# A linear-attention and mixture kernel: the state update's products spread over all four quarters of TensorE's array

## The chip, the cores and the metric

The kernel runs on one core of a Trainium2 chip. The metric is the device time of one launch in microseconds (us), as the median of several runs. The engines are TensorE (PE in the rows, with PEld for its weight loads), VectorE (DVE), ScalarE (ACT), GpSimd (POOL) and SyncE (SP), which here only issues transfers. Each engine works through a stream of its own in a fixed order and waits on semaphores for the others.

## The reference, cut to what matters

Three parts follow each other. The first is a recurrence over 768 tokens for 4 batches (b) and 8 heads (h), with a 48x48 state for each of the 32 pairs:

```python
for t in range(S):                       # S = 768, D = 48
    kt, vt, bt = (k_n[:, :, t], v[:, :, t], beta[:, :, t, None])
    y[:, :, t] = np.einsum('bhd,bhde->bhe', q[:, :, t], state)
    v_old = np.einsum('bhde,bhd->bhe', state, kt)
    state = state + bt[:, :, :, None] * np.einsum('bhd,bhe->bhde', kt, vt - v_old)
```

Its output, 3072 rows of 384, goes through `h = (x @ w1) * (x @ w2) @ w3` and `h @ w_out` (width 1024), and then through a soft mixture of 8 experts with 4 slots each: softmax over the tokens, two expert matrices, softmax over the slots. Everything is float32 in the reference.

## The kernel before

**Tiling of the recurrence.** The 768 tokens are 24 chunks n of 32 tokens; two neighbours form a pair c (12 pairs). Within a chunk the recurrence is solved as a triangular system (`solve_steps`, mostly VectorE); from chunk to chunk the state is carried. `chain_steps(n)` (lines 579 to 648) holds the steps of one chunk, in this order: `pre` (GpSimd scales v), `ks` (L599, keys times state, then a subtraction on VectorE, L601), `vv` (L610, the solved system times v, then four ScalarE copies, L575, into the tile `sv`), `yy` (L620, queries times state, output `yp`, copied by ScalarE, L623), `ss` (L630, only in the second chunk of a pair, and not in the last pair: 11 times in all) and `xt` (L642, transposes for the next part).

**The state.** `sv` has 128 rows and a block of 384 columns (8 heads of 48) for each batch. Batches 0 and 1 keep their state in rows 64 to 111, batches 2 and 3 in rows 0 to 47 (`srow`); the other rows hold the chunk's solved v, of batches 0 and 1 in rows 0 to 63 and of batches 2 and 3 in rows 64 to 127. The sum of the state itself stays in two accumulators of PSUM, `sacc[0]` for batches 0 and 2 and `sacc[1]` for batches 1 and 3. `ss` adds 32 products to them (4 batches, 8 heads, each 64 rows deep with 48 columns in and out), and then ScalarE copies each batch's part of the accumulator into its rows of `sv` (four copies of 48x384, L575). One product in the program is two weight loads and two matmuls in the trace, so `ss` is 64 records of each.

**A product's place in the array.** A product that reads rows 0 to 63 uses the upper half of the array's rows, one that reads 64 to 127 the lower half; its output rows in PSUM, 0 to 47 or 64 to 111, set which half of the columns it uses. So a quarter of the array is a pair of such halves. `yy` and `vv`, by contrast, write 32 output rows for each batch, so that the four batches take four strips of 32 columns.

**The work around it.** `main_steps(c)` runs the two big matrices on the 64 tokens of a pair: `prod` (L695, output `ab`, 18 matmuls of 128x256 for each of 8 blocks), ScalarE and VectorE (L699, L704) for the product of both, `gtr` (L712) transposes, then logits, softmax and sums (L719 to L798). In the first 205 us VectorE, ScalarE and GpSimd also convert the weights w1, w2, w3 and w_out from 64-bit to 32-bit pieces (L290 to L307), and TensorE multiplies w3 and w_out with phi (L322 to L356). After about 580 us comes a tail with the experts.

**What sets the order.** The steps are entered with due times (`when`, `spread`, a table `SHIFT`), and a scheduler that simulates the engines then decides each engine's order from the dependencies. A step that takes another time in its simulation, or waits for something else, can move its neighbours.

Of the kernel before, what the change touches and what calls it, by code (L numbers as in the profile page):

```python
# [19 lines left out]
B, H, S, D = 4, 8, 768, 48  # L20
# [3 lines left out]
NCH = NST // 2  # L24
# [96 lines left out]
def kern(ctx, tc, kq, vt, kt, bl, w12, w3, wo, phi, w1e, w2e, consts, out):  # L121
    nc = tc.nc
    V, A, G, T = nc.vector, nc.scalar, nc.gpsimd, nc.tensor
# [25 lines left out]
    def at(name):  # L149
        return bank("at", 2, name)  # L150
# [23 lines left out]
    sv = px.tile([128, 4, H * D], F32, name="sv")  # L174
    sacc = [ps.tile([128, 512], F32, name=f"sacc{i}") for i in range(2)]
# [19 lines left out]
    def kl_of(p):  # L195

        i = p if p < 3 else (0, 1, 3, 2)[(p - 3) % 4]
        return held4 if i == 3 else kls[i]
# [27 lines left out]
    def srow(b):  # L226

        return slice(64, 112) if b < 2 else slice(0, 48)

    def qrow(b):  # L230
        return slice(32 * b, 32 * b + 32)

    def trow(n, b):

        return qrow(b if n % 2 else b ^ 1)

    def kcol(h, b):
        return slice(64 * h + 32 * (b % 2), 64 * h + 32 * (b % 2) + 32)
# [171 lines left out]
    def g_step(n, hs, which="gp"):  # L410

        s, n4 = divmod(n, 4)
        if n4 == 0 and "g" in which and hs[0] == 0:
            Dg[s] = pk.tile([128, 32, 32], F32, tag="L", name=f"dg{s}", bufs=NL)
        t = kl_of(n // 2)
        k = [(3, 3), (5, 1)][n % 2]

        span = {"gp": [((3, 7), (0, 4)), ((5, 7), (0, 2))], "g": [((3, 4), (3, 4)), ((5, 6), (1, 2))],
                "p": [((4, 7), (0, 3)), ((6, 7), (0, 1))]}[which][n % 2]
        nb = span[0][1] - span[0][0]  # L420
        p = (ab if n // 4 == 1 else at)(f"{which}{n}_{hs[0]}")
        gp = p[:, 0:len(hs) * nb * 32].rearrange("p (h k i) -> p h k i", h=len(hs), k=nb)
        for h in hs:
            for b in range(4):
                r, kc, j = srow(b), kcol(h, b), b // 2
                lo, hi = span[j]
                slots = slice(lo, hi) if j == 0 else slice(hi - 1, lo - 1 if lo else None, -1)
                T.matmul(gp[trow(n, b), h - hs[0]], lhsT=t[r, k[j], kc], rhs=t[r, slots, kc], start=True, stop=True)  # L428
        blocks = {}
        if "g" in which:  # L430
            blocks["g"] = 0
        if "p" in which:
            blocks["p"] = o = len(which) - 1
            blocks["x"] = o + 1
        g_evac(n, hs, gp, blocks, n < PP)
# [134 lines left out]
    def copy(n, b, o, i):  # L570

        if n < NSPLIT and b % 2:
            V.tensor_copy(o, i)
        else:
            A.copy(o, i)  # L575

    def chain_steps(n):
        s, n4 = divmod(n, 4)
        c, t2 = divmod(n, 2)
        st = {}  # L580
        kl = kl_of(n // 2)

        def pre():
            v = KV[n]
            G.tensor_tensor(out=v, in0=v, in1=nnT[s][:, 8 * n4:8 * n4 + 8].unsqueeze(2).to_broadcast([128, H, D]),  # L585
                            op=ALU.mult)

        def rows(b):
            return slice(0, 112) if b < 2 else slice(0, 128)

        def ks():

            v = KV[n]
            p = at(f"ks{n}")
            kp = p[:, 0:384].rearrange("p (h d) -> p h d", h=H)
            for h in range(H):
                for b in range(4):
                    r, o = (rows(b) if t2 else srow(b)), trow(n, b)
                    T.matmul(kp[o, h], lhsT=kl[r, (5, 1)[b // 2] if t2 else 3, kcol(h, b)],  # L599
                             rhs=sv[r, b, h * D:(h + 1) * D], start=True, stop=True, tile_position=(r.start, o.start))  # L600
            V.tensor_tensor(out=v, in0=v, in1=kp, op=ALU.subtract)  # L601

        def vv():
            r, w = KV[n], W[s]
            assert s not in HALVES or n4 in joined[s]
            p = at(f"vp{n}")
            for h in range(H):
                for b in range(4):
                    o = qrow(b)
                    T.matmul(p[o, h * D:(h + 1) * D], lhsT=w[o, 8 * n4 + h, :], rhs=r[o, h, :],  # L610
                             start=True, stop=True, tile_position=(o.start, o.start))
            for b in (0, 2, 1, 3):
                copy(n, b, sv[trow(n, b), b, :], p[trow(n, b), 0:384])

        def yy():
            p = at(f"yp{n}")
            for h in range(H):
                for b in range(4):
                    r = trow(n, b) if n == 0 else rows(b)
                    T.matmul(p[qrow(b), h * D:(h + 1) * D], lhsT=kl[r, (6, 0)[b // 2] if t2 else (4, 2)[b // 2], kcol(h, b)],  # L620
                             rhs=sv[r, b, h * D:(h + 1) * D], start=True, stop=True, tile_position=(r.start, 32 * b))
            ys = px.tile([128, DM], F32, tag="ys", name=f"ys{n}", bufs=2)
            A.copy(ys, p[:, 0:384])  # L623
            st["y"] = ys

        def ss():
            k = KK[c]
            for h, b in [(h, b) for b2 in range(2) for h in range(H) for b in (b2, b2 + 2)]:
                r = slice(64 * (b // 2), 64 * (b // 2) + 64)
                T.matmul(sacc[b % 2][srow(b), h * D:(h + 1) * D], lhsT=k[r, b % 2, h, :],  # L630
                         rhs=sv[r, b, h * D:(h + 1) * D], start=False, stop=(c == NCH - 2),
                         skip_group_check=True, tile_position=(r.start, 64 - 64 * (b // 2)))
            for b in (0, 2, 1, 3):
                copy(n, b, sv[srow(b), b, :], sacc[b % 2][srow(b), 0:384])

        def xt():
            ys = st["y"]
            if t2 == 0:
                xT[c] = [pl["xt"].tile([128, 3, 2, 128], F32R, tag="xT", name=f"xT{c}_{i}", bufs=4) for i in range(2)]
            p = (at if n < NXT else tr)(f"xp{n}")  # L640
            for k in range(3):
                T.transpose(p[:, k * 128:(k + 1) * 128], ys[:, k * 128:(k + 1) * 128], ident)  # L642
            xh, xl = xT[c]
            pv = p[:, 0:384].rearrange("p (k t) -> p k t", k=3)
            A.copy(xh[:, :, t2, :], pv)  # L645
            V.tensor_tensor(out=xl[:, :, t2, :], in0=pv, in1=xh[:, :, t2, :].bitcast(F32), op=ALU.subtract)  # L646

        return [pre] + [ks] * (n > 0) + [vv, yy] + [ss] * (t2 and c < NCH - 1) + [xt]
# [272 lines left out]
    for c in range(NCH):  # L921
        a, b, p = main_steps(c)
# [117 lines left out]
    for hf in range(2):  # L1040
        p = ab(f"h1p{hf}")
        for f in range(8):
            q = 32 * (f % 4)
            T.matmul(p[q:q + 32], lhsT=uT[:, f % 4, f // 4, :], rhs=w3s[hf][f],
                     start=(f < 4), stop=(f >= 4), skip_group_check=True)
# [19 lines left out]
    for f in range(8):  # L1065
        q = 32 * (f % 4)
        m = T.matmul(p[q:q + 32, 0:384], lhsT=h1T[:, f, :], rhs=wos[:, f, :], start=(f < 4), stop=(f >= 4),
                     skip_group_check=True)
    load_w2(nfree + 4, nlate)
    si = u4[:, 0:DM]  # L1070
    for k in range(3):
        c = slice(k * 128, (k + 1) * 128)
# [201 lines left out]
```

## Time and profile before

| | before |
|---|---|
| time, median of 3 runs | 643.93 us (643.07 to 649.51) |
| the profiled execution: its time / its span | 642.53 / 640.7 us |
| TensorE busy: matmuls / weight loads | 548.9 / 458.8 us |
| VectorE, ScalarE, GpSimd busy | 400.3, 278.6, 161.8 us |
| mean granted TensorE clock | 0.946 |

A group of equal instructions has its busy time, the mean duration of one, and the idle time of its engine just ahead of it with what ended that. A matmul's duration in the records is its latency, and several are in flight at once: what a group costs the engine is read from the time between its first start and the next group's start. In the timeline, a row is a run of equal instructions: its start, its length, the engine and line, output and inputs, and the count.

### The profile page before, as it was taken

How to read it: one execution, taken by the hardware profiler on the slowest of the kernel's cores; microseconds unless marked ns; L12 is line 12 of the kernel's file. 1: busy time of each engine (PE TensorE's matmuls, PEld its weight loads, DVE VectorE, ACT ScalarE, POOL GpSimd, SP SyncE). 2: the span in 40 equal slices, each digit the busy share in tenths (PEclk: the TensorE clock that was granted, in tenths of full speed). 3: DMA queues.
4: the chain of work that ended last, by engine and by line, in shares of the span. 5: the costliest groups of instructions: out<-in, count | busy, mean ns of one | idle time of the engine just before them, and what ended most of it. 6: DMA issues, size and time to landing. Idle time of an engine off the chain costs nothing.

```text
span 640.7 us, 25996 instructions
## 1 busy us (share of the span) xinstructions
PE 548.9 (86%) x11417; PEld 458.8 (72%) x11417; DVE 400.3 (62%) x1257; ACT 278.6 (43%) x704; POOL 161.8 (25%) x215
## 2 busy tenths in 40 slices
PE   5324546888899799899999999897999999999996
PEld 4323435887777688679888888786989899886464
DVE  3996899998667115994379826997982313134124
ACT  1515644245574436454444455343444454333023
POOL 0726858334254016232030113004010000000100
PEclk9999666598999989999999999999999999999997
DMA  9904234446843720310404030122344130788848
GB/s 205 332 4 146 81 83 144 130 130 204 254 151 129 164 70 17 87 45 18 105 7 96 9 90 30 38 61 63 106 145 155 63 108 2 268 274 318 344 160 265
DMA packets 36945, 81.72 MB, mean 128 GB/s; under 512 B 4352, under 2 KB 17792, under 8 KB 35584
## 3 DMA queue, kind: packets, MB, share of 16 engines
q1 hardware_dynamic: 36832, 80.07, 40.9%
q8 instruction: 89, 1.46, 1.0%
q14 instruction: 24, 0.20, 0.1%
HBM read 69.57 MB, written 10.49 MB: 125 GB/s over the span
## 4 chain that ended last, share of the span: by engine, by line
PE 55%; DVE 26%; issue 6%; DMA 5%; POOL 4%; ACT 3%; SPq 0%; DVEq 0%; POOLq 0%; ACTq 0%
PE ab L695 24%; DMA kl<-kq 4%; PE gp L712 3%; PE yp L620 3%; DVE xl L512 2%; PE vp L610 2%; DVE tmp L509 2%; PE sacc L630 2%; PE gp L428 2%; PE ks L599 2%; PE sacc L1119 2%; PE hp L1098 2%; DVE gl L454 2%; DVE xl L487 1%; PE lp L719 1%
## 5 line engine op out<-in xcount | busy, mean ns | idle before, releaser
L695 PE MATMUL ab<-xT,wsl 128*128 128x256 f32 x1728 | 247.1, 296 | 3.6 <-DVE gT L704 2.2
L695 PEld LDWEIGHTS ab<-xT,wsl 128*128 128x128 f32 x1728 | 221.8, 196 | 15.6 <-issue 6.3
L704 DVE TENSOR_TENSOR gT<-ab,bs 128x256 f32<-128x256 f32 x84 | 35.2, 422 | 87.3 <-ACT bs L699 79.0
L699 ACT COPY bs<-ab 128x256 f32<-128x256 f32 x96 | 35.7, 371 | 68.0 <-PE ab L695 66.3
L585 POOL TENSOR_TENSOR v<-v,nnT 128x384 f32<-128x384 f32 x24 | 21.4, 894 | 139.2 <-DMA v<-vt 57.0
L575 ACT COPY sv<-vp 32x384 f32<-32x384 f32 x96 | 45.1, 470 | 16.2 <-PE vp L610 14.5
L512 DVE TENSOR_TENSOR xl<-xl,tmp 128x84 f32<-128x84 f32 (+35 forms) x220 | 51.5, 266 | 0.7
L509 DVE TENSOR_TENSOR tmp<-xl 128x84 f32<-128x84 f32 (+35 forms) x220 | 49.6, 259 | 0.4
L428 PE MATMUL gp<-kl 48*32 48x64 f32 (+1 forms) x1024 | 35.7, 275 | 11.7 <-ACT kl L408 8.6
L299 POOL TENSOR_TENSOR hold<-hold 128x384 f32<-128x384 f32 (+1 forms) x32 | 32.7, 1025 | 47.9 <-DVE hold L296 23.0
L428 PEld LDWEIGHTS gp<-kl 48*32 48x32 f32 x1024 | 26.1, 121 | 17.8 <-ACT kl L408 8.9
L713 ACT COPY gtok<-gp 128x512 f32<-128x512 f32 x48 | 28.2, 588 | 17.2 <-PE gp L712 15.0
L393 POOL TENSOR_TENSOR kl<-praw,cs 64x256 f32<-64x256 f32 x28 | 25.3, 903 | 33.5 <-ACT praw L384 32.3
L620 PE MATMUL yp<-sv,kl 112*32 112x48 f32 (+2 forms) x1280 | 26.3, 215 | 7.6 <-ACT sv L575 7.6
L291 ACT ACTIVATE hold<-hold,cs 128x384 int32<-128x384 int32 (+1 forms) x32 | 18.7, 589 | 27.7 <-DVE hold L290 27.3
L408 ACT COPY kl<-gp 32x256 f32<-32x256 f32 x64 | 23.2, 363 | 15.0 <-DVE kl L393 11.8
L620 PEld LDWEIGHTS yp<-sv,kl 112*32 112x32 f32 (+2 forms) x1280 | 20.4, 115 | 12.2 <-issue 8.4
L610 PE MATMUL vp<-v,w 32*32 32x48 f32 x1536 | 25.3, 207 | 3.1 <-DVE mst L738 0.9
L646 DVE TENSOR_TENSOR xT<-xp,xT 128x384 fp32r<-128x384 f32 x24 | 13.3, 553 | 22.8 <-ACT xT L645 22.6
L610 PEld LDWEIGHTS vp<-v,w 32*32 32x32 f32 x1536 | 20.1, 107 | 10.2 <-issue 6.0
L712 PE MATMUL gp<-cs,gT 128*128 128x128 f32 x168 | 26.9, 279 | 0.0
L400 POOL TENSOR_TENSOR kl<-praw,cs 32x256 f32<-32x256 f32 x28 | 23.2, 828 | 7.7 <-ACT praw L384 4.8
(248 smaller groups left out, 980.6 us busy)
## 6 DMA issues: line engine op xcount, KB each, us to landing
hold<-w SPq DMA_DIRECT2D x16, 384.0 KB, 3.3
v<-vt SPq DMA_DIRECT2D x24, 192.0 KB, 2.7
kk<-kt SPq DMA_DIRECT2D x12, 384.0 KB, 6.7
unitg<-w1e SPq DMA_DIRECT2D x6, 768.0 KB, 5.7
kl<-kq SPq DMA_DIRECT2D x8, 512.0 KB, 6.8
kl<-kq SPq DMA_DIRECT2D x8, 384.0 KB, 4.6
gx<-w SPq DMA_DIRECT2D x4, 768.0 KB, 8.2
raw_w<-w SPq DMA_DIRECT2D x4, 768.0 KB, 8.8
```

The costliest lines, as they stand in the source:

```text
L299: G.tensor_tensor(out=w, in0=m, in1=w, op=ALU.mult)
L428: T.matmul(gp[trow(n, b), h - hs[0]], lhsT=t[r, k[j], kc], rhs=t[r, slots, kc], start=True, stop=True)
L509: V.tensor_tensor(out=tmp[:, 0:n, lo:hi], in0=x[:, j + 1:32, j:j + 1].to_broadcast([128, n, hi - lo]), in1=x[:, j:j + 1, lo:hi].to_broadca ...
L512: V.tensor_tensor(out=x[:, j + 1:32, lo:hi], in0=x[:, j + 1:32, lo:hi], in1=tmp[:, 0:n, lo:hi], op=ALU.add)
L575: A.copy(o, i)
L610: T.matmul(p[o, h * D:(h + 1) * D], lhsT=w[o, 8 * n4 + h, :], rhs=r[o, h, :], start=True, stop=True, tile_position=(o.start, o.start))
L620: T.matmul(p[qrow(b), h * D:(h + 1) * D], lhsT=kl[r, (6, 0)[b // 2] if t2 else (4, 2)[b // 2], kcol(h, b)], rhs=sv[r, b, h * D:(h + 1) * D ...
L695: T.matmul(o, lhsT=w[:, m, k], rhs=x[:, k], start=(n == 0), stop=(n == 8))
L699: A.copy(bs, p[:, 256:512])
L704: V.tensor_tensor(out=gt, in0=p[:, 0:256], in1=bs, op=ALU.mult)
L712: T.transpose(p[:, t * 256 + i * 128:t * 256 + (i + 1) * 128], gt[:, t * 128:(t + 1) * 128], ident)
L713: A.copy(gk, p)
```

## The change

```diff
+    def arow(b):
+
+        return srow(b if b % 2 == 0 else 3 - b)
...
         def ss():
             k = KK[c]
-            for h, b in [(h, b) for b2 in range(2) for h in range(H) for b in (b2, b2 + 2)]:
-                r = slice(64 * (b // 2), 64 * (b // 2) + 64)
-                T.matmul(sacc[b % 2][srow(b), h * D:(h + 1) * D], lhsT=k[r, b % 2, h, :],
-                         rhs=sv[r, b, h * D:(h + 1) * D], start=False, stop=(c == NCH - 2),
-                         skip_group_check=True, tile_position=(r.start, 64 - 64 * (b // 2)))
+            for h in range(H):
+                for b in (0, 2, 1, 3):
+
+                    r, o = slice(64 * (b // 2), 64 * (b // 2) + 64), arow(b)
+                    T.matmul(sacc[b % 2][o, h * D:(h + 1) * D], lhsT=k[r, b % 2, h, :],
+                             rhs=sv[r, b, h * D:(h + 1) * D], start=False, stop=(c == NCH - 2),
+                             skip_group_check=True, tile_position=(r.start, o.start))
             for b in (0, 2, 1, 3):
-                copy(n, b, sv[srow(b), b, :], sacc[b % 2][srow(b), 0:384])
+                copy(n, b, sv[srow(b), b, :], sacc[b % 2][arow(b), 0:384])
```

Before, batches 0 and 1 used the quarter (upper rows, right columns) and batches 2 and 3 the quarter (lower rows, left columns), and all products of `sacc[0]` stood ahead of those of `sacc[1]`. Now batch 1 is summed in rows 0 to 47 of `sacc[1]` and batch 3 in rows 64 to 111, so they use the two quarters that stood idle, and the four batches of a head are entered one after the other. The ScalarE copies of batches 1 and 3 read one half of the partitions and write the other. Number and size of products and copies stay as they were. Lines behind the insertion move down by four, behind the loop by six (L630 is L636, L620 is L624, L695 is L701).

The scheduler makes the following of it. The first place is `ss` of pair 8 on TensorE (the names end in numbers: `kk_6997` are the keys of that pair, `sacc_109` is `sacc[0]`, `sacc_110` is `sacc[1]`; x16 is 16 products). Before:

```order
L620 MATMUL yp_7482<-sv,kl_112 32x48
L630 MATMUL sacc_109<-sv,kk_6997 48x48 x3
L620 MATMUL yp_7482<-sv,kl_112 32x48 x2
L630 MATMUL sacc_109<-sv,kk_6997 48x48
L620 MATMUL yp_7482<-sv,kl_112 32x48 x29
L630 MATMUL sacc_109<-sv,kk_6997 48x48 x12
L630 MATMUL sacc_110<-sv,kk_6997 48x48 x16
L642 MATMUL xp_7583<-cs,ys_7515 128x128 x3
```

The same place now:

```order
L624 MATMUL yp_7482<-sv,kl_112 32x48
L636 MATMUL sacc_109<-sv,kk_6997 48x48 x4
L624 MATMUL yp_7482<-sv,kl_112 32x48 x31
L636 MATMUL sacc_110<-sv,kk_6997 48x48 x4
L636 MATMUL sacc_109<-sv,kk_6997 48x48 x2
L636 MATMUL sacc_110<-sv,kk_6997 48x48 x2
L636 MATMUL sacc_109<-sv,kk_6997 48x48 x2
L636 MATMUL sacc_110<-sv,kk_6997 48x48 x2
L636 MATMUL sacc_109<-sv,kk_6997 48x48 x2
```

The pattern of two and two goes on to the end of `ss`, 24 products in all: pairs on one diagonal of quarters alternate with pairs on the other. Pairs 9 and 10 read the same.

The second place is `ss` of pair 1 on TensorE, while w3 is still being multiplied with phi (`w3tw`). Before:

```order
L630 MATMUL sacc_109<-sv,kk_1288 48x48 x5
L343 MATMUL w3tw_1725<-cs,hold 128x128 x3
L630 MATMUL sacc_109<-sv,kk_1288 48x48 x9
L356 MATMUL w3tw_1685<-cs,part_1657 128x32
L630 MATMUL sacc_109<-sv,kk_1288 48x48
```

Now:

```order
L636 MATMUL sacc_109<-sv,kk_1288 48x48 x5
L347 MATMUL w3tw_1725<-cs,hold 128x128 x3
L636 MATMUL sacc_109<-sv,kk_1288 48x48 x9
L360 MATMUL w3tw_1685<-cs,part_1657 128x32
L636 MATMUL sacc_109<-sv,kk_1288 48x48
```

Nothing moved here: one accumulator is still filled almost whole ahead of the other, because the products of batches 0 and 2 are ready earlier. Pair 0 reads the same before and now. So 9 of the 11 `ss` have the two-and-two pattern, over 24 of 32 products in most (27 in pair 4, 24 in pair 2, 16 in pair 6).

The third place is `ss` of pair 2 on TensorE and what follows it (`j` are products of the solve, `gp` transposes of `gtr`). Before:

```order
L630 MATMUL sacc_109<-sv,kk_2552 48x48 x5
L620 MATMUL yp_3002<-sv,kl_113 32x48 x32
L630 MATMUL sacc_109<-sv,kk_2552 48x48 x10
L630 MATMUL sacc_110<-sv,kk_2552 48x48 x16
L642 MATMUL xp_3096<-cs,ys_3035 128x128 x3
L542 MATMUL j_2_3124<-w_1419,dg_906 32x16 x32
L712 MATMUL gp_1_3230<-cs,gx 128x128 x4
...
L712 MATMUL gp_2_3356<-cs,gx 128x128
L550 MATMUL j_2_3125<-t_2_3158,sums 32x16 x32
L542 MATMUL j_3_3259<-w_1419,dg_906 32x16 x32
```

Now, behind the last pair of `ss`:

```order
L648 MATMUL xp_3096<-cs,ys_3035 128x128 x3
L546 MATMUL j_2_3124<-w_1419,dg_906 32x16 x32
L701 MATMUL ab_6_3193<-xT_0_2064,wsl_106 128x256
...
L718 MATMUL gp_0_3217<-cs,gx 128x128 x4
L718 MATMUL gp_1_3230<-cs,gx 128x128 x4
...
L554 MATMUL j_2_3125<-t_2_3158,sums 32x16 x32
L701 MATMUL ab_7_3236<-xT_0_2064,wsl_107 128x256 x2
...
L546 MATMUL j_3_3259<-w_1419,dg_906 32x16 x32
```

Here `ss` moved ahead of half a block of `prod` (9 matmuls of `ab_6`) and of `gp_0`, and the two blocks of `j` that stood side by side now have part of another `prod` between them. This is the place where the order differs most; from pair 4 on the differences are a few matmuls of `prod` at a time.

## Rows read from the trace of the kernel before

**Rows 1.** The page: busy time by engine, and the chain's shares.

```profile
PE 548.9 (86%) x11417; PEld 458.8 (72%) x11417; DVE 400.3 (62%) x1257; ACT 278.6 (43%) x704; POOL 161.8 (25%) x215
...
PE 55%; DVE 26%; issue 6%; DMA 5%; POOL 4%; ACT 3%; SPq 0%; DVEq 0%; POOLq 0%; ACTq 0%
```

**Rows 2.** Windows: stretch, length, each engine's busy time (instructions), clock, DMA share, GB/s.

```profile
100.00:200.00 100.00, 87.43 (x1649) 73.54 (x1641) 86.32 (x245) 48.36 (x117) 44.02 (x45) 0.86 0.57 174
200.00:300.00 100.00, 92.09 (x2185) 77.25 (x2177) 57.51 (x203) 50.06 (x134) 32.53 (x52) 0.97 0.29 73
300.00:400.00 100.00, 97.69 (x2235) 85.94 (x2234) 60.44 (x216) 47.99 (x122) 15.53 (x41) 1.00 0.24 55
400.00:500.00 100.00, 94.28 (x1997) 82.36 (x1995) 75.90 (x312) 42.97 (x105) 12.44 (x24) 1.00 0.31 93
```

**Rows 3.** Waits of TensorE, 200 to 560 us: total, times, longest.

```profile
PE j L550 <- issue: 3.0, 1, 3.0
...
PE gp L428 <- DMA kl<-kq: 1.1, 2, 0.6
```

**Rows 4.** Timeline around `ss` of pair 4: start, length, what, count.

```profile
306.28 0.25 PEld L630 LDWEIGHTS sacc<-sv,kk 64*48 64x48 f32 x6
...
307.01 0.73 PEld L620 LDWEIGHTS yp<-sv,kl 128*32 128x32 f32 x58
...
307.81 1.34 PEld L630 LDWEIGHTS sacc<-sv,kk 64*48 64x48 f32 x56
...
308.60 1.97 ACT L575 COPY sv<-sacc 48x384 f32<-48x384 f32 x4
...
309.20 1.01 PEld L695 LDWEIGHTS ab<-xT,wsl 128*128 128x128 f32 x8
...
313.26 0.75 PEld L599 LDWEIGHTS ks<-sv,hold 48*32 48x32 f32 x64
```

**Rows 5.** Timeline: a run of products with 16 columns.

```profile
217.36 0.60 PEld L542 LDWEIGHTS j<-w,dg 32*32 32x32 f32 x61 [0.60 <-issue]
```

**Rows 6.** Chain that ended last, 60 to 560 us: start, length, what.

```profile
214.91 1.30 PE sacc L630 x52
...
218.65 2.16 PE ab L695 x18
...
226.57 3.84 PE ab L695 x18
...
268.77 7.21 DMA kl<-kq
...
307.88 1.39 PE sacc L630 x56
...
318.17 1.90 DVE gl L454
...
366.04 0.88 PE vp L610 x59
...
378.86 1.39 PE sacc L630 x56
...
414.70 6.18 DMA kl<-kq
...
455.16 1.39 PE sacc L630 x56
...
485.94 1.39 PE sacc L630 x56
...
517.39 1.39 PE sacc L630 x56
```

**Rows 7.** Windows around an idle stretch of all engines, columns as in rows 2.

```profile
216.00:218.00 2.00, 1.50 (x78) 1.15 (x73) 0.10 (x1) 1.83 (x5) 0.30 (x1) 1.00 1.10 225
...
222.00:224.00 2.00, 0.00 (x0) 0.00 (x0) 0.00 (x0) 0.00 (x0) 0.00 (x0) 0.94 0.00 2
...
226.00:230.00 4.00, 4.00 (x21) 4.00 (x19) 0.00 (x0) 0.69 (x2) 0.00 (x0) 0.50 0.00 0
```

**Rows 8.** The ScalarE copies of line 575: shortest/median/longest ns.

```profile
L575 ACT COPY sv<-vp x96: 462/470/474, 51.4 to 544.1; 32x384 f32<-32x384 f32 x96
L575 ACT COPY sv<-sacc x44: 472/473/476, 81.8 to 519.6; 48x384 f32<-48x384 f32 x44
```

## The prediction

> **What bounds the kernel now.** I read first the page's busy times and chain [rows 1]: TensorE is busy 86% of the span and holds 55% of the chain, VectorE 26%. Those are averages over different stages, so the second view is the table of windows [rows 2]. From 100 to 200 us both engines are near full (TensorE 87.43, VectorE 86.32 of 100): there a gain on one alone is not yet a gain in time. From 300 to 400 us TensorE has 97.69 of 100 and VectorE 60.44; from 200 to 300 and 400 to 500 it has 92.09 and 94.28. So for most of the recurrence behind 200 us TensorE's stream sets the pace, and a microsecond less work in it is up to a microsecond less time.
>
> "Up to", since TensorE also meets VectorE's triangular solves and late transfers there. The third view is the chain in order of time [rows 6]. A group of the changed line L630 stands on it where the time of `ss` decides the end. I find it in pair 2 (214.91), 4 (307.88), 6 (378.86), 8 (455.16), 9 (485.94) and 10 (517.39). In pair 3 the chain goes over the load of keys at 268.77 (7.21 us), and TensorE later waits for such loads, though never over 0.6 us [rows 3]. In pair 5, between those of pairs 4 and 6, it runs on VectorE from the transpose at 318.17 to the vp products at 366.04. In pair 7 it goes over the load at 414.70. Pairs 0 and 1 lie ahead of 162 us.
>
> **The change part by part.** *The products.* What does one `ss` cost? In pair 4 [rows 4] the 58 records of `yp` start at 307.01 and `ss` behind them at 307.81: 0.80 us, 13.8 ns each. The 56 records of `ss` start at 307.81 and the next group at 309.20: 1.39 us, 24.8 ns each. Both have 48 columns to stream; `yp` spreads over four strips of columns, `ss` over two quarters. The floor lies lower: 61 records with 16 columns take 0.60 us [rows 5], 9.8 ns. So with four quarters at work I expect about `yp`'s pace, 11.0 ns less for each record. Bounds: nothing, if two quarters over the same half of the columns cannot run at once (no row shows such a pair, since `yp`'s strips never share columns); and 24.8 − 9.8 = 15.0 ns at the floor. I take 11.0, because `yp` has the same length of stream.
>
> [...]
>
> How many records go faster? The change acts where the scheduler puts pairs on both diagonals side by side. In pairs 0 and 1 it does not: one accumulator is filled almost whole first, so the gain there is nothing. In pairs 8, 9 and 10 it is 24 of 32 products, in pair 2 also 24, in pair 4 27 and in pair 6 16. On the chain that is 24+27+16+24+24+24 = 139 products, 278 records, and 278 × 11.0 ns = 3.06 us. Pairs 3, 5 and 7 have about 24 + 24 + 24 products more, 144 × 11.0 ns = 1.6 us of TensorE time, that I count at nothing: behind them TensorE meets a load or the solve a little later than it comes, and would only wait longer. If that cover is thinner than it looks, these 1.6 us come on top. With the bounds, the term runs from 0 to (278 + 144) × 15.0 ns = 6.3 us.
>
> *The copies.* Before, the copies out of `sacc[0]` could start when half of `ss` was done; now both accumulators end together. In pair 4 the first copy starts at 308.60, 0.79 us behind the start of the 56 records. At the new pace the whole of `ss` needs 8 × 24.8 + 48 × 13.8 ns = 0.86 us, so the first copy starts within 0.1 us of where it did. The copies end at 310.57 (308.60 + 1.97), and the next reader, `ks`, starts at 313.26: 2.7 us of slack [rows 4]. Behind the four copies on ScalarE stands the bs copy for `prod`, which is no later either. Should the products not speed up, `ss` ends at 309.20 as now, and the first copy starts some 0.65 us later, still inside that slack.
>
> The copies of batches 1 and 3 now cross from one half of the partitions to the other. No row shows such a copy. The two kinds there are, 32 and 48 rows, take 470 and 473 ns [rows 8], so the number of rows does not matter; I take the crossing at nothing. A copy at twice the time would add 2 × 0.47 = 0.95 us for a pair, inside the slack of 2.7.
>
> *Transfers.* The next keys are loaded when `yp` has been read, and `yp` stands ahead of most of `ss`; the load of the other keys (`kk`) waits for the end of `ss` and is wanted a whole pair later. Neither has a price.
>
> *The scheduler's shuffle.* Between 150 and 260 us the order changes most, around `ss` of pair 2. Just behind this place the trace has a hole: all engines stand still from 222 to 224 us [rows 7], and TensorE's wait at `j` is put down to nothing that the profile shows, 3.0 us [rows 3]. Transfers had filled the 16 DMA engines in the stretch ahead (share 1.10 from 216 to 218) and were over by 222. [...] In the new order the work behind `ss` is nearly the same: 32 `j` products, 17 `prod` matmuls and 8 transposes instead of 18 and 5, then `j` again. So I expect the hole to stay, and count nothing. Bounds: minus 5.5 us if it goes, plus 5.5 for each new one.
>
> **The sum.** 642.53 (the profiled execution) − 3.1 = 639.4 us. The median of the runs shown, 643.93, stands 1.4 us above that execution, so on its scale I predict 640.8 us, 0.5% less. A difference under 1% (6.4 us) is about what a measurement of this kernel cannot tell from no change.
>
> **The rivals.** *A. No gain in the products.* Two quarters over the same columns exclude each other, or each product has a fixed cost. For it: no row has two products share a half of the columns. Against the fixed cost: 9.8 ns in rows 5. It gives 643.9 us. [...]
>
> *B. The hole behind pair 2 goes.* For it: its place depends on what stands between a burst of transfers and two dense blocks of `j`, and these blocks stand apart now. Against it: the burst is released by the same `yp`. It gives 640.8 − 5.5 = 635.3 us; with the 1.6 us of pairs 3, 5 and 7, 633.7.
>
> *C. A new hole, on the other side.* TensorE goes through `yp` and `ss` faster, 0.80 + 0.86 us instead of 2.19, right when the loads of the next keys start. If what stopped it at 221 us is that instructions come too late for dense runs of small products, a denser `ss` can stop in one of the 9 places. For it: rows 7, and that the hole opens inside a run at about 10 ns a record. Against it: no other such wait is on the list behind 200 us except that of 3.0 us [rows 3]. One hole with its slow clock costs 5.5 us: 646.3 us, slower than before. From two holes on, 651.8 us, it is slower by over 1%.
>
> **How the numbers follow.** The forecast has a chance of 0.52 (639 to 642.5 us by itself), A 0.17, B 0.16, C with one hole 0.10, with two 0.05. The range from 635.0 to 646.5 us takes in the forecast, A, one hole and the greater part of B. Faster by over 1% (under 637.5 us) is B and the edge of the forecast, where pairs 3, 5 and 7 count and the pace is nearer the floor: 0.16 + 0.07 = 0.23. Slower by over 1% (over 650.4) is C with two holes and a little for what I have not seen: 0.07. The rest, 0.70, is no change that can be told.
>
> **What would show it.** In the new trace the group of `ss` behind `yp` in pairs 8 to 10 should take 0.8 to 0.9 us from its start to the next group, against 1.39; at 1.3 or more, A holds. The copies of line 575 should stay at 473 ns. The first copy should start as far behind `yp` as before. Waits of TensorE behind 200 us that nothing explains, with a clock of 0.50 after them, decide between B and C: the one at 221 us gone, or new ones. If the products do reach 13.8 ns and the time is still the same, then the waits for loads or for VectorE must have grown by as much, and my reading of the six places on the chain was wrong; if the time falls by 5 us or more without any hole gone, pairs 3, 5 and 7 counted.

## The result and the profile after

The kernel became slower. Over 20 runs of each, the changed kernel takes 648.71 us and the kernel before 644.27 us in the median; the ratio is 1.0069, with a 95% interval of 1.0044 to 1.0094. The forecast was 640.8 us in a range of 635.0 to 646.5. The ratios here and below compare the fast runs of both kernels alone, so they are not exactly the quotients of the medians beside them. The profiled execution of the changed kernel has a span of 646.9 us against 640.7.

The page after, where [rows 1] stood:

```profile
PE 552.5 (85%) x11417; PEld 460.3 (71%) x11417; DVE 402.2 (62%) x1257; ACT 278.9 (43%) x704; POOL 165.4 (26%) x215
...
PE 47%; DVE 30%; issue 7%; DMA 6%; POOL 5%; ACT 4%; SPq 0%; DVEq 0%; POOLq 0%; ACTq 0%
```

TensorE's share of the chain fell from 55% to 47%. Half of what it lost went to VectorE (26% to 30%), and one point each to transfers, GpSimd, ScalarE and time that nothing explains.

The four quarters themselves do what was expected of them. The timeline of TensorE in pair 10 of the changed kernel (start, length, what, count):

```profile
523.29 0.88 PE L624 MATMUL yp<-sv,kl 112*32 112x48 f32 x62
524.10 0.92 PE L636 MATMUL sacc<-sv,kk 64*48 64x48 f32 x56
524.96 0.55 PE L648 MATMUL xp<-cs,ys 128*128 128x128 f32 x3
525.26 3.36 PE L701 MATMUL ab<-xT,wsl 128*128 128x256 f32 x26
528.54 0.28 PE L603 MATMUL ks<-sv,kl 48*32 48x48 f32 x6
528.76 0.33 PE L718 MATMUL gp<-cs,gT 128*128 128x128 f32 x1
529.02 0.86 PE L603 MATMUL ks<-sv,kl 48*32 48x48 f32 x58
529.82 0.55 PE L718 MATMUL gp<-cs,gT 128*128 128x128 f32 x3
530.12 1.08 PE L701 MATMUL ab<-xT,wsl 128*128 128x256 f32 x7
```

The 56 records of `ss` hold TensorE from 524.10 to 524.96, 0.86 us or 15.4 ns each, where they held it 1.39 us [rows 4, 6]. The difference, 0.53 us, is 48 records at 11.0 ns, as forecast. But the same rows show most of the gain going again. In the kernel before, the place behind it read:

```profile
522.30 0.89 PE L599 MATMUL ks<-sv,kl 48*32 48x48 f32 x64
523.11 0.66 PE L712 MATMUL gp<-cs,gT 128*128 128x128 f32 x4
523.53 1.19 PE L695 MATMUL ab<-xT,wsl 128*128 128x256 f32 x8
```

From the start of `ks` to the next `prod` it was 1.23 us; now the scheduler has put one transpose of `gp` inside `ks`, and it is 1.58, so 0.35 of the 0.53 us is gone.

The copies, where [rows 8] stood, kept their time:

```profile
L579 ACT COPY sv<-sacc x44: 470/473/478, 83.6 to 526.5; 48x384 f32<-48x384 f32 x44
```

The first of them starts 2.23 us behind the first `yp` record of pair 10, where it was 2.12 us.

TensorE's waits from 200 to 560 us, where [rows 3] stood (total, times, longest):

```profile
PE j L554 <- issue: 3.6, 1, 3.6
PE ab L701 <- DVE gT L710: 3.2, 3, 1.7
PE gp L432 <- DMA kl<-kq: 1.8, 2, 0.9
PE gp L432 <- DMA hold<-kq: 1.7, 1, 1.7
```

The hole at `j` is 0.6 us longer than the 3.0 of before, and the waits for keys (`kl`, `hold`) went from 1.1 and 0.7 us to 1.8 and 1.7. Behind these longer waits, at 355 and 427 us, the granted clock stays at 1.00 (windows as in rows 2):

```profile
320.00:360.00 40.00, 37.58 (x838) 32.70 (x836) 33.52 (x133) 18.11 (x47) 6.13 (x19) 1.00 0.21 49
...
400.00:440.00 40.00, 36.30 (x798) 31.94 (x796) 36.99 (x155) 16.08 (x44) 5.42 (x11) 1.00 0.18 41
```

### The profile page after: what moved, and what is told of

The parts are those of the page before. It is cut to its first block, busy times and chain, and to the rows that moved or that the text cites. A ratio compares the mean times of both kernels' runs of the same rounds, so it can differ in the third digit from the quotient of the medians.

```text
span 646.9 us, 25996 instructions
## 1 busy us (share of the span) xinstructions
PE 552.5 (85%) x11417; PEld 460.3 (71%) x11417; DVE 402.2 (62%) x1257; ACT 278.9 (43%) x704; POOL 165.4 (26%) x215
## 3 DMA queue, kind: packets, MB, share of 16 engines
q8 instruction: 89, 1.46, 0.9%
## 4 chain that ended last, share of the span: by engine, by line
PE 47%; DVE 30%; issue 7%; DMA 6%; POOL 5%; ACT 4%; SPq 0%; DVEq 0%; POOLq 0%; ACTq 0%
PE ab L701 20%; DVE tmp L513 4%; DVE xl L516 4%; DMA kl<-kq 3%; PE yp L624 3%; PE gp L718 2%; PE gp L432 2%; DMA hold<-w 2%; PE vp L614 2%; PE sacc L1125 2%; PE ks L603 2%; PE hp L1104 2%; DVE xl L491 1%; PE sacc L636 1%; DVE hold L294 1%
## 5 line engine op out<-in xcount | busy, mean ns | idle before, releaser
L701 PE MATMUL ab<-xT,wsl 128*128 128x256 f32 x1728 | 251.4, 297 | 3.3 <-DVE gT L710 3.2
L701 PEld LDWEIGHTS ab<-xT,wsl 128*128 128x128 f32 x1728 | 223.6, 197 | 16.5 <-issue 6.7
L432 PE MATMUL gp<-kl 48*32 48x64 f32 (+1 forms) x1024 | 37.1, 279 | 11.8 <-ACT kl L412 7.9
L303 POOL TENSOR_TENSOR hold<-hold 128x384 f32<-128x384 f32 (+1 forms) x32 | 34.6, 1086 | 46.4 <-DVE hold L300 24.4
L624 PE MATMUL yp<-sv,kl 128*32 128x48 f32 (+2 forms) x1280 | 27.3, 219 | 6.6 <-ACT sv L579 6.6
L624 PEld LDWEIGHTS yp<-sv,kl 128*32 128x32 f32 (+2 forms) x1280 | 20.9, 117 | 11.6 <-issue 8.0
L614 PE MATMUL vp<-v,w 32*32 32x48 f32 x1536 | 26.7, 216 | 1.9 <-DVE w L556 0.9
L614 PEld LDWEIGHTS vp<-v,w 32*32 32x32 f32 x1536 | 21.7, 114 | 8.4 <-issue 5.1
```

Source lines behind the costliest of these rows:

```text
L303: G.tensor_tensor(out=w, in0=m, in1=w, op=ALU.mult)
L701: T.matmul(o, lhsT=w[:, m, k], rhs=x[:, k], start=(n == 0), stop=(n == 8))
```

## The experiments

Two things changed at once: where the products stand, and, through the scheduler, the order of the engines' streams. To part them, the order was pinned: behind the traced kernel, edges that set the issue order alone tie each instruction to the one ahead of it in a recorded list, for all five engines. The pin is no change of its own: with a kernel's own order and no other edit, the built program has the same instructions with the same waits as without it, for the kernel before and for the changed one.

```diff
         kern(tc, *args, o)
+        pin(tc)
...
+        for a, b in zip(names, names[1:]):
+            tc.add_manual_dep(by[b], a, mybir.DependencyInfo(mybir.DependencyClass.NoSync, ...))
```

**Order alone, quarters alone.** The first kernel has the order of the changed kernel and the old quarters; the second the order of before and the four quarters, with the 32 places of each `ss` filled head after head. The diff is that of the first against the changed kernel; the second has none but its list.

```diff
-                    r, o = slice(64 * (b // 2), 64 * (b // 2) + 64), arow(b)
+                    r, o = slice(64 * (b // 2), 64 * (b // 2) + 64), srow(b)
...
-                copy(n, b, sv[srow(b), b, :], sacc[b % 2][arow(b), 0:384])
+                copy(n, b, sv[srow(b), b, :], sacc[b % 2][srow(b), 0:384])
```

> Every engine issues in exactly the order of the changed kernel, but the products stand in the two old quarters and the copies come out of the old rows. Theory (the order eats the gain): the order costs what the change lost plus what the products save, 4.4 + 3 = about 7 us, so 651 us, 1.011 of the kernel before; ss takes 1.3 to 1.4 us a pair again. Rival (the four quarters themselves cost something, such as the crossing copies or the later first copy): then the order is harmless and this kernel takes the time of before, 644 us, ratio 1.000.

> Every engine issues in exactly the order of the kernel before; only the places that the products of ss hold among themselves are filled with head after head over the four quarters, and the copies come out of the new rows. Theory (the order eats the gain): the products save their 3.1 us and nothing is lost, 641 us, ratio 0.995, with ss at 0.85 to 0.9 us a pair. Rival (the four quarters cost something): about the time of after, ratio 1.005 or more.

The first took 649.49 us, ratio 1.0084 (1.0052 to 1.0117); the second 643.81, ratio 0.9998 (0.9970 to 1.0027). The order theory holds: the order by itself costs about 5.4 us (3.3 to 7.5). But half of the second expectation failed: even in the old order the four quarters bring nothing. The trace says where they are lost. The starts of the `vp` groups, trace against trace, come 0.70, 0.68, 0.70, 0.69 and 0.68 us earlier from one side of `ss` to the other in pairs 4, 6, 8, 9 and 10: here all 32 products alternate, and 64 records at 11.0 ns are 0.70. In two places that is more than given back: 2.6 us between pairs 5 and 6 and 2.2 us between pairs 7 and 8. TensorE behind pair 5, first in the kernel before, then with the four quarters:

```profile
348.88 0.41 PE L428 MATMUL gp<-hold 48*32 48x128 f32 x4
350.01 0.96 PE L428 MATMUL gp<-hold 48*32 48x128 f32 x26 [0.72 <-DMA hold<-kq]
...
350.83 0.93 PE L599 MATMUL ks<-sv,kl 48*32 48x48 f32 x58
351.68 2.41 PE L695 MATMUL ab<-xT,wsl 128*128 128x256 f32 x18
353.93 0.60 PE L712 MATMUL gp<-cs,gT 128*128 128x128 f32 x4
```

```profile
341.37 0.84 PE L636 MATMUL sacc<-sv,kk 64*48 64x48 f32 x56
...
346.65 0.41 PE L432 MATMUL gp<-hold 48*32 48x128 f32 x4
348.92 1.71 PE L432 MATMUL gp<-hold 48*32 48x128 f32 x26 [1.85 <-DMA hold<-kq]
...
350.46 1.66 PE L603 MATMUL ks<-sv,kl 48*32 48x48 f32 x58
352.05 4.04 PE L701 MATMUL ab<-xT,wsl 128*128 128x256 f32 x18
355.92 0.60 PE L718 MATMUL gp<-cs,gT 128*128 128x128 f32 x4
```

TensorE comes to `gp` earlier, but the keys are loaded only when `yp` has been read, and the 512 KB of them land 6.5 us (before) and 7.0 us (here) after their issue. So it waits 1.85 us instead of 0.72. Behind that wait the granted clock is 0.50: `ks` takes 1.59 us to the next group instead of 0.85, 18 matmuls of `prod` 3.87 instead of 2.25. The windows of the second kernel (stretch, length, busy times of the five engines, clock, DMA share, GB/s):

```profile
345.00:347.00 2.00, 2.00 (x19) 1.66 (x17) 2.00 (x10) 0.73 (x2) 0.00 (x0) 1.00 1.03 215
...
351.00:353.00 2.00, 2.00 (x54) 1.88 (x45) 2.00 (x10) 0.72 (x2) 0.00 (x0) 0.50 0.03 8
```

**The wait by itself.** If that is the cause, the kernel before, with none of the change, must lose time when its keys come later. Here the loads of the keys in pairs 5 and 7 wait for the last product of `ss` instead of `yp`; `LATE` lists such pairs of instructions (numbers in the code, names in the diffs below), and `pin` ties them with a true dependency.

```diff
+    for dma, mm in LATE:      # kq of pairs 5 and 7 <- last matmul of ss of the same pair
+        tc.add_manual_dep(by["I-%d" % dma], "I-%d" % mm, mybir.DependencyInfo(mybir.DependencyClass.Sync, ...))
```

> The kernel before with its old quarters; only the loads of the keys in pairs 5 and 7 start behind the last product of ss instead of behind yp, some 1.4 us later. Theory: gp waits 1.8 to 2.2 us instead of 0.7 in these two places, the granted clock falls to 0.50 behind each, and each place loses 2.5 to 4 us of TensorE's time, of which 1 to 2 vanish in later waits for VectorE: 646 to 649 us, ratio 1.004 to 1.009. Rival (the wait itself is all, the clock keeps up): each place loses 1.4 us less what later waits absorb, 644 to 645.5 us, ratio 1.000 to 1.003.

It took 651.51 us, ratio 1.0105 (1.0066 to 1.0145): 6.8 us, more than expected. Its trace lost 4.5 us at the first place and 5.1 at the second, 9.6 in all; a trace is one execution, and the runs of one kernel lie some 5 us apart, so such a reading does not replace the ratio. At the first place the keys come 2.35 us later: from the start of the last 58 records of `yp` to the second group of `gp` it is 10.18 us, where it was 7.83 in the kernel before.

```profile
342.91 0.87 PE L620 MATMUL yp<-sv,hold 128*32 128x48 f32 x58
...
350.54 0.41 PE L428 MATMUL gp<-hold 48*32 48x128 f32 x4 [0.87 <-DMA hold<-kq]
353.09 1.58 PE L428 MATMUL gp<-hold 48*32 48x128 f32 x26 [2.14 <-DMA hold<-kq]
...
354.50 1.65 PE L599 MATMUL ks<-sv,kl 48*32 48x48 f32 x58
356.09 4.17 PE L695 MATMUL ab<-xT,wsl 128*128 128x256 f32 x18
```

The waits here grew by 2.3 us (0.87 + 2.14 − 0.72); behind them `ks` takes 1.59 us and the 18 matmuls of `prod` 4.01, with the granted clock at 0.50 from 356 to 358 us. So a longer wait for the keys is enough, and it can cost more than its length. It is not certain each time: the changed kernel waited 1.7 us behind pair 5, at 355 us, and its clock was 1.00 from 320 to 360 us.

**The loads of `kk`.** The next theory was that the keys land late because the load of `kk`, released by the end of `ss`, runs beside them. In four kernels it is held back in pairs 2 to 7: in pair 2 until the first `prod` group of that pair, then until the first `gp` group that reads the new keys.

```diff
+LATE = [kk3 <- ab2_0, kk4 <- gp14_0, kk5 <- gp16_0, kk6 <- gp18_0, kk7 <- gp20_0, kk8 <- gp22_0]
```

> Four quarters in the order of the kernel before, with the load of kk held back in pairs 2 to 7 until the first group of gp that reads the next keys (in pair 2 until the first prod group), so that the keys, which gp waits for, have the transfer engines to themselves. Theory (the products do save 0.7 us a pair, but TensorE only comes earlier to the same load, waits longer, and pays a stretch at the lower clock for the longer wait): without that wait the gain shows, 634 to 638 us, ratio 0.985 to 0.992, and waits of gp for kl and hold under 1 us in all. Rival (the time saved on TensorE is given back to VectorE's solves or elsewhere, the loads are only where it shows): the time stays at 642 to 644 us, ratio 0.997 to 1.000, and VectorE's waits grow instead.

> The kernel before with nothing changed but the loads of kk held back in the same way. It waits for the keys only 1.8 us in all and has one hole of 3.0 us with 6.8 us at the lower clock behind it, so it gains less: both theories expect 639 to 642 us, ratio 0.993 to 0.998. The difference to the kernel with four quarters and the same loads tells them apart: 4 to 6 us by the theory of the loads, about 0 by the rival.

> The changed kernel in its own order with the loads of kk held back in pairs 2 to 7. Theory: it too waits for keys and has the hole, so it gains 3 to 6 us on after, 643 to 646 us, ratio 0.999 to 1.004; what is left against the kernel with four quarters in the old order, about 5 us or more, is the price of the order by itself. Rival (the order costs nothing without the waits): about the same time as four quarters in the old order, 0.986 to 0.992.

> The old quarters in the order of the changed kernel with the loads of kk held back in pairs 2 to 7: the fourth corner. Theory of the loads: 4 to 6 us more than four quarters in the same order with the same loads, about 648 us, ratio 1.006. Rival: the same time as four quarters in that order.

| | old quarters | four quarters |
|---|---|---|
| old order | 1 (before) | 0.9998 |
| new order | 1.0084 | 1.0069 (after) |
| old order, `kk` late | 0.9962 (0.9934 to 0.9990) | 0.9911 (0.9882 to 0.9940) |
| new order, `kk` late | 1.0050 (1.0031 to 1.0069) | 1.0024 (0.9999 to 1.0049) |

Each time is near what was expected for it, but the differences are not, and the mechanism fails. With four quarters in the old order, TensorE still waits 1.7 and 2.1 us for the keys, whose 512 KB land 6.9 and 7.2 us after their issue: they are no sooner without `kk` beside them, so it was not `kk` that slowed them. The trace loses 0.9 and 2.1 us at the two places. What the late `kk` does shorten is the unexplained waits behind pair 2 (below), from 3.5 to 2.2 us with the old quarters and from 4.2 to 3.2 with the new ones, both in the old order. With it, the four quarters are worth 3.3 us in the old order (0.0051 of 644) and 1.7 in the new one, each with an uncertainty of about 2, where 4 to 6 were expected; the order costs 5.7 and 7.3 us. In the new order without this edit, the changed kernel against the first kernel above, the ratios give 1.0 us, and the traces 0.64, 0.54, 0.54 and 0.53 us in pairs 4, 8, 9 and 10 and nothing in pair 6.

**The wait covered.** Here, with `kk` late and the old order, the 18 matmuls of `prod` that stood behind the waiting `gp` in pairs 5 and 7 go ahead of it, with their ScalarE copy; once with four quarters and once with the old ones.

```diff
-    pair 5:  gp18_0 x16, ks12 x32, ab5_0 x18        pair 7:  gp22_0 x16, ab6_7 x18
+    pair 5:  ab5_0 x18, gp18_0 x16, ks12 x32        pair 7:  ab6_7 x18, gp22_0 x16
```

> Four quarters, order of before and late kk (638.8 us), but in pairs 5 and 7 the next prod group of 18 matmuls goes ahead of the gp products that wait for the new keys (with its bs copy on ScalarE ahead of the copies out of gp). Theory (the longer waits of 1.7 and 2.1 us for the keys and the lower clock behind them eat what the products save): both waits lie under the prod group, the granted clock stays at full speed there, and 2 to 4 us more come out: 634.5 to 637 us, ratio 0.985 to 0.989. Rival (VectorE's solve ends just behind, so that TensorE would wait there instead): 638 to 640 us, 0.990 to 0.993, with vp waiting for VectorE by as much as gp did for the keys.

> The old quarters with late kk and with prod ahead of gp in pairs 5 and 7: what is left against the same kernel with four quarters (640.2 us, 0.9934) is what the products are worth once TensorE no longer waits for the keys. Theory: 2.5 to 4 us more than it, ratio 0.997 to 0.999. Rival (the products are worth nothing on the whole): the same, 0.993.

With four quarters: 640.18 us, ratio 0.9934 (0.9908 to 0.9959). With the old ones: 643.25, ratio 0.9992 (0.9961 to 1.0023). The waits for keys are gone from both places, and behind pair 5 of the first kernel `ks` takes 0.79 us and the 18 matmuls of `prod` 2.35, but that kernel brings nothing over 0.9911 and misses the 634.5 to 637 us expected. TensorE's waits with the four quarters now read

```profile
PE ab L701 <- DVE gT L710: 1.6, 2, 1.2
PE vp L614 <- DVE sm L465: 1.5, 1, 1.5
PE vp L614 <- DVE mst L744: 1.2, 1, 1.2
```

so VectorE takes over a part, as the rival said. What this pair of kernels gives is the worth of the products: 0.0058 or 3.7 us, with an uncertainty of about 2.6 (the two ratios come from different chips). Trace against trace `ss` brings 0.67 to 0.83 us in pairs 4, 6, 7, 8, 9 and 10 and nothing in pair 5, 4.3 us in all, with no loss behind pairs 5 and 7; another 1.7 us between 437 and 450 us come from a longer wait for `gT` (1.9 us) in the trace with the old quarters.

**The hole behind pair 2.** In the traces of seven kernels (before and changed, the four quarters in the old order, the old quarters with `kk` late in both orders, and two of those below) TensorE's unexplained waits between 205 and 240 us begin at one of three places in the order of its matmul records, about no. 3524, 3652 or 3906 (each within three). The first two are 128 apart and the third is twice that, within two, behind the second; 128 records of matmuls with as many weight loads are 256 instructions. The transfers of the queue for instructions (q8) are 89 packets with 1.46 MB, 16 KB each; 89 times 256 are 22784, and TensorE has 22834 instructions. And in five of these traces, at the longest such wait (1.6 to 3.6 us), TensorE goes on 1.3 to 1.5 us after the end of one of these packets. The transfers in the kernel before, first from 216.0 to 221.8 us, the last 0.4 us of which lie in the hole, then from 221.8 to 222.5 (queue and kind: packets, MB, share of 16 engines):

```profile
q1 hardware_dynamic: 265, 1.25, 97.2%
...
q8 instruction: 1, 0.02, 9.2%
```

In these rows no instruction packet comes through while the burst (1.25 MB) lasts; the first starts when it ends, at 221.89 us, and takes 1.03 us, and TensorE goes on at 224.38. Two kernels had only the first line of that list, `kk3 <- ab2_0`, which shortens the burst by 384 KB: the changed kernel in its own order, and the four quarters in the order of before.

> The changed kernel in its own order, but the load of kk for pair 3 (384 KB) waits for the first prod group of pair 2 instead of the end of ss, so that the burst of transfers behind pair 2 is shorter by that load. Theory (TensorE stands still because its next block of instructions is fetched behind that burst): the fetch ends about 1.9 us earlier, the hole of 3.6 us shrinks to under 1.7 us or goes, and the granted clock behind it does not fall to 0.50: 3 to 6 us less than after, ratio to before 0.998 to 1.002. Rival (the hole comes from the dense products themselves, or from the clock): hole and clock stay, ratio 1.007 as after.

> The order of the kernel before, the four quarters, and the load of kk for pair 3 behind the first prod group of pair 2. If both theories hold their gains add: 3.1 us for the products and 3 to 5.5 us for the hole with its slow clock, 636 to 638 us, ratio 0.987 to 0.990. If only the order theory holds 0.995; if only the fetch theory holds about 1.000; if neither, 1.005 or more.

The second took 642.15 us, ratio 0.9963 (0.9931 to 0.9995), short of the 636 to 638 us expected if both gains added. Its packet starts at 219.95 instead of 221.75 us in the same kernel with the early `kk`, 1.8 us sooner, and the wait shrank from 3.5 us by about as much:

```profile
220.38 0.58 PE L554 MATMUL j<-t,sums 32*32 32x16 f32 x47
222.56 0.33 PE L554 MATMUL j<-t,sums 32*32 32x16 f32 x17 [1.61 <-issue]
```

But waits of 1.2 and 1.0 us now stand at the two other places, where there was one of 0.7, so that all of them together fell only from 4.2 to 3.8 us. The first kernel took 647.41, ratio 1.0052 (1.0023 to 1.0081), against 0.998 to 1.002 expected: there the wait moved to another block of `j` (L546 instead of L554) and was 4.6 us long. Two more kernels moved the keys of pair 6 away as well: until `ab1_7` had been issued, and (with `prod` ahead of `gp` in pairs 5 and 7) until the end of `ab2_0`.

```diff
+LATE += [kl for pair 6 <- ab1_7]                        first kernel
+LATE += [kl for pair 6 <- ab2_0], kk3 <- gp12_0         second kernel
```

> Four quarters, order of before and late kk (638.8 us), and the load of the keys of pair 6 (896 KB, wanted only at some 240 us) is also held back, from the end of yp of pair 2 until the prod group ab1_7 has been issued, some 5 us later. Theory (TensorE's own instructions are fetched behind the burst): the fetches ahead of the j products start on time, the waits of j and ks that nothing explains (1.9 and 1.2 us) are under 0.5 us each, the clock behind 210 us does not fall, and 2 to 4 us come out: 634.5 to 637 us, ratio 0.985 to 0.989. Rival (the hole belongs to the j products or moves with any transfer): a hole of 1.5 us or more is still between 210 and 240 us, 638 to 640 us.

> Four quarters, order of before, prod ahead of gp in pairs 5 and 7, and behind pair 2 the load of the next keys held back until the prod group ab2_0 (226 us) and kk until gp of chunk 12 (240 us), so that no burst of transfers lies over the j products. Theory of the instruction fetch: only the first of the unexplained waits is left (at 217 us, behind an older burst, 1.3 to 1.9 us), or one at ks (231 us) under the moved burst; 634 to 638 us, ratio 0.984 to 0.990. Rival (the hole just moves with the burst and costs as much): 640 us, 0.993, as without this edit.

They took 640.86 us, ratio 0.9938 (0.9909 to 0.9966), and 640.74, ratio 0.9936 (0.9908 to 0.9964): nothing gained over the kernels without this edit. In the first, waits of 1.2 and 1.5 us are left at `j`. In the second the `j` products run without a hole, with 18 matmuls of `prod` between them in 2.24 us, and the wait stands at `ks`, under the burst that now lies from 228.2 us to beyond 231.5; the packet came through inside it, at 230.72 us:

```profile
220.92 2.40 PE L701 MATMUL ab<-xT,wsl 128*128 128x256 f32 x18
...
223.92 0.72 PE L546 MATMUL j<-w,dg 32*32 32x16 f32 x62
...
230.71 0.65 PE L603 MATMUL ks<-sv,kl 48*32 48x48 f32 x41
233.53 0.70 PE L603 MATMUL ks<-sv,kl 48*32 48x48 f32 x23 [2.17 <-issue]
```

So the theory of the instruction fetch is borne out by where the waits begin, 256 instructions apart or about twice that, by the packet of 16 KB ahead of the end of those in five traces, and by their moving with the burst; the edit is no cure, and the rival's forecast of the time was right.

**Where the order costs.** The order of before up to the `vp` of chunk 9 (302 us) and the new one behind it, and the reverse, both with four quarters:

> Four quarters, original loads; every engine issues in the order of the kernel before up to the vp products of chunk 9 (302 us there) and in the order of the changed kernel from there on. With the old order throughout the four quarters took 643.8 us, with the new one 648.7. If the order costs mostly where it differs most, in the first 300 us with the j products and the conversion of w3, this takes 643 to 645 us (ratio 0.999 to 1.002); if it costs behind it, where pairs 7 to 10 are cut into more pieces, 647 to 649 (1.005 to 1.008); if evenly, 646.

> The counterpart: the order of the changed kernel up to the vp products of chunk 9, the order of the kernel before from there on. If the order costs in the first 300 us: 647 to 649 us (1.005 to 1.008); if behind: 643 to 645 (0.999 to 1.002); if evenly 646. The profiles with old quarters put 2.6 us of 6.7 ahead of that place, which speaks for evenly.

Ratios 1.0033 (1.0006 to 1.0061) and 1.0022 (0.9990 to 1.0054), 646.81 and 647.30 us beside 645.48 for before on that chip, against 0.9998 with the old order throughout: as far as these intervals tell, both halves cost, about evenly. One thing that differs in many places is where runs of small products are cut. Counted in the built programs, the order of before changes 338 times between matmuls over the whole array and smaller ones, the new order 344 times; from the first `vp` product of chunk 5 on it is 251 and 265. One kernel puts a price on a cut: before, with three matmuls of a neighbouring `prod` issued singly inside each of 18 runs, 54 cuts.

```diff
-    ks12 x32, ab5_0 x18
+    ks12 x8, ab5_0, ks12 x8, ab5_0, ks12 x8, ab5_0, ks12 x8, ab5_0 x15
```

> The kernel before, with nothing changed but this: in 18 runs of 32 small products (ks, vp and yp of chunks 7 to 22) three matmuls of the neighbouring prod group are issued one by one inside the run, 54 cuts. Theory (each change between small products and matmuls over the whole array costs TensorE 0.15 to 0.2 us, two of them a cut): each such run takes 0.9 to 1.2 us longer and the kernel 10 to 18 us, ratio 1.015 to 1.028, some of it hidden in waits; then the 15 extra changes of the new order cost 2 to 3 us of its 5. Rival (cuts cost next to nothing, the order loses by its waits): under 3 us, ratio below 1.005.

It took 656.40 us, ratio 1.0190 (1.0149 to 1.0231): 12.3 us, 0.23 us for a cut. One such run, with `prod` at 0.127 us a matmul behind it (15 in 1.90 us; 18 in 2.25 at the same place before):

```profile
355.46 0.41 PE L599 MATMUL ks<-sv,kl 48*32 48x48 f32 x10
355.80 0.38 PE L695 MATMUL ab<-xT,wsl 128*128 128x256 f32 x1
356.12 0.38 PE L599 MATMUL ks<-sv,kl 48*32 48x48 f32 x16
356.42 0.38 PE L695 MATMUL ab<-xT,wsl 128*128 128x256 f32 x1
356.74 0.37 PE L599 MATMUL ks<-sv,kl 48*32 48x48 f32 x16
357.04 0.39 PE L695 MATMUL ab<-xT,wsl 128*128 128x256 f32 x1
357.36 0.38 PE L599 MATMUL ks<-sv,kl 48*32 48x48 f32 x16
357.66 2.06 PE L695 MATMUL ab<-xT,wsl 128*128 128x256 f32 x15
```

Uncut, `ks` took 0.85 us and three matmuls of `prod` take 0.4; here it is 2.20, so 0.32 us for each cut where nothing hides it. By these prices the 6 to 14 extra changes, 3 to 7 cuts, are by estimate 0.7 to 2.2 us of the order's 5; the expectation, with 15 changes, put them at 2 to 3. The trace gives the price; what TensorE does at such a change, no row shows.

Another part shows in TensorE's waits behind 195 us, with the old quarters in both orders, first that of before, then the new one:

```profile
PE ab L695 <- DVE gT L704: 2.2, 2, 1.8
...
PE ab L701 <- DVE gT L710: 4.1, 3, 1.7
```

TensorE waits once more for VectorE's `gT`, at 452 us. With four quarters it is 3.6 us in all where the second half has the new order and 2.9 where it has the old one. The rest of the order's cost is not settled: the traces put most of what lies in the first half between 150 and 245 us, where work on w3 moves in among the products of pairs 1 and 2, but no run took a single one of these moves alone, nor the wait for `gT`.

## Why the prediction was wrong

*The products' term was right in size for one `ss`.* 11.0 ns for each record that goes faster: 0.53 us for 24 products in the changed kernel, 0.70 for 32 in the old order. As a sum on the chain, 3.1 us is within the uncertainty of what the four quarters are worth in the old order, 3.7 us where the wait for the keys is covered and 3.3 with `kk` late; but there all 32 products alternate and pair 7 counts. In the new order, for which it was forecast, the traces show 2.3 us without pair 2 and the runs 1.0 and 1.7. Rival A, no gain in the products, falls: 56 records in 0.86 us are 15.4 ns each.

*The copies* cost what they did and start where they did, as forecast.

*"I count them at nothing" failed for pairs 5 and 7, in the old order.* The step said that behind pairs 3, 5 and 7 TensorE "would only wait longer". There it does wait longer, and behind pair 5 then runs at a clock of 0.50: 1.1 us more of waiting and 18 matmuls in 3.87 us instead of 2.25. The price was not zero but 2.6 and 2.2 us, and it took the whole gain of the other pairs. In the changed kernel's own trace the waits for keys are 1.7 us longer in all, but the clock stays at 1.00 behind them, so there the step is off by the waits alone. The reading under it was short as well: "never over 0.6 us" holds for the keys in `kl`; behind pair 5 TensorE waited 0.72 us for `hold` already. The forecast had the price of a slow stretch in hand, from the hole [rows 6, 7], and used it for holes alone. The line on transfers, "Neither has a price", belongs to the same error: the 512 KB of keys land 6.2 to 7.3 us after their issue (pairs 5 and 7, before and with four quarters in the old order), and what shortens the work inside that time lengthens the wait.

*The scheduler's shuffle, "count nothing", failed, and is the larger part.* With old quarters the new order costs 5.4 us, and this is why the change made the kernel slower. The measured time is 7.9 us above the forecast: by estimate 5.4 for the order and 2.1 for the part of the products' 3.1 us that did not arrive in it, each with an uncertainty of 2 to 3. The forecast looked for one hole more or less and found none; it had no price for cuts, for one more wait for `gT`, or for the many small moves ahead of 245 us. What in the order costs most stays open. The forecast had called the stretch before 200 us one where a gain on one engine alone is not yet a gain in time, and did not ask what a loss there is.

*The hole behind pair 2 stayed*, as expected, and B and C did not come as described. No run shows the 5.5 us that the bounds and these rivals put on a hole: the kernel before shows 3.0 us of waiting and 18 matmuls that take 1.7 us more at the clock of 0.50 behind it [rows 3, 6, 7], the changed kernel 3.6 us of waiting and the clock at 0.50 from 228 to 231 us. That it comes from instructions arriving late was C's guess; that the burst ahead holds them up was B's. The packets and waits above fit both.

*The step that would have shown it* was named: products at their pace and the time unchanged would mean that waits for loads had grown by as much. In the old order that is what the trace has, 3.2 us more of waiting for keys, and behind pair 5 the clock of 0.50.

The best versions found keep the old order, use the four quarters and hold `kk` back: 638.83 us, ratio 0.9911, or 640.18, ratio 0.9934, with `prod` ahead of `gp`. Both beat the kernel before and the changed kernel; between the two the runs do not decide.

## What to carry to other kernels

Time saved ahead of a wait is not always merely lost: where TensorE's clock falls behind the longer wait, that place can cost more than the saving (2.6 us here behind pair 5, with the clock at 0.50, for 0.7 saved), so the wait has to be covered together with the saving. When an edit goes through a scheduler, pin the old order and measure the edit in it, and then measure the new order with the old code; here the order cost 5.4 us, more than the edit was worth in any of the orders. A run of small products that another shape cuts paid 0.2 to 0.3 us here for each cut, what 20 to 30 records of `ss` saved.

## What was not expected of the hardware

Instructions come in while the kernel runs, 89 packets of 16 KB that fit TensorE's count and take 1.0% of the time of the 16 transfer engines, and TensorE stood still for 1.6 to 3.6 us where one of these packets came behind or inside a burst of loads, in a dense run of small products. Waits for keys that grew by 2.3 us cost the kernel before 4.5 us in one place of a trace, with the clock at 0.50 behind them; a wait of 1.7 us left it at 1.00 in the changed kernel. And filling the two idle quarters, each of which shares a half of the columns and a half of the rows with the quarters in use, did pay: 24.8 ns a record became 15.4. Which of the quarters run at once, no run here separates.
